# Retention, spectral mixing and a gated MLP: a new planned order, fewer warm-up products, packed state

## The chip, the cores and the metric

One NeuronCore of one Trainium2 chip runs the whole program. The metric is device microseconds of one execution; the kernel before took 392.88 us as the median of three runs (392.62 to 393.3). The engines named below are TensorE (PE, with its weight loads as PEld), VectorE (DVE), ScalarE (ACT), GpSimd (POOL) and SyncE (SP, which issues the DMAs).

## The reference, cut to what matters

All arrays are fp32. There are 2 sequences of 768 tokens, 8 heads of 64, and a model width of 512.

```
state = gamma * state + outer(k_t, v_t); y_t = scale * q_t @ state      # per head, 768 steps
theta = x @ w_theta; zr, zi = x*cos(theta), x*sin(theta)
u = x + w_tok_r @ zr + w_tok_i @ zi                                     # mixes the tokens
x2 = u + relu(u @ w_ch)
h = gelu(x2 @ w_in); a, v = halves(h)
out = x2 + (a * (w_sg @ layernorm(v) + b_sg)) @ w_out                   # w_sg mixes the tokens
```

## The kernel before, in words

**Tiling.** The retention is done in 12 chunks of 128 tokens (6 per sequence). Within a chunk the scores of all 8 heads are products of 64 rows (heads 2p and 2p+1 in the two row halves), masked by the decay on VectorE; what came before the chunk enters through a state of 64 by 64 per head. Two heads make one 128 by 128 block of `state`, of which only the two diagonal 64 by 64 blocks are filled and the rest is zero from a memset; four such blocks lie in a tile of 128 by 512, and two tiles take turns. `outer` makes the new k-v products, `grow` adds them to the state (two VectorE operations, one per half of the partitions), `fade_k` multiplies k by its decay on GpSimd and a second GpSimd product makes the faded q (`qd`). `attend` multiplies the state with `qd` (four products of 128 by 128) and adds the masked scores times v (eight products with 64 columns of weights).

**Later stages.** Each chunk then gets its angles (`theta`), cosines and sines, and joins the token mixing (`mix_main` for the first 512 tokens, `mix_rest` for the last 256). After all chunks come three dense layers over three groups of tokens: group 0 and 1 are the first 512 tokens of each sequence, group 2 the last 256 of both. In the gated MLP, `up_v`, `norm` and `up_u` run group after group; `gate_tile` of a sequence needs the normalised v of all its tokens, so of its own group and of group 2.

**Precision.** Wide products are made in three passes from a high and a low part of each operand. So every operand is split: ScalarE copies the high part (line 302), VectorE subtracts it (line 308). The 19 weight tiles come as raw 64-bit words of 1 MB; each is decoded by a ScalarE scaling (line 361), a VectorE shift (370), two VectorE passes (381), and a split. Raw tiles have two buffers (`RAWS`), so the third weight load waits until the first tile is split. fp32 products of the retention appear in the trace as two halves each; the wide products of split operands as one instruction each.

**What sets the order.** All engines run a fixed order, written by a planner (`Plan.schedule`). It keeps a clock for each engine and for the DMA queue, a price per operation, and a priority (due time); at each step it takes the engine that can start first, and on it the ready operation with the best priority among those that start within a small window (`PEL` 0.3 for TensorE). `SP` loads are priced at KB/410 us each on one queue, plus 2.0 until landing. An operation may not start more than `AHEAD` before its priority. In `C`, `SGP` says how much earlier than the first gating product the gating weights `wsg` get their priority. Operations on VectorE and GpSimd that work on SBUF alone exclude each other in the plan (`port`).

**Warm-up and fillers.** Before the planned program, 11 products of a state tile with itself are issued (`warm`). In the plan, up to 90 filler products on `ident` (`keep_warm`) are offered to TensorE; the planner puts one in where TensorE has nothing else ready, and drops those that would start after 34 us of planned time.

Where the planner starts its clocks:

```
engines = {o.eng: 0.0 for o in self.ops}
state = {"port": 0.0, "dma": 0.0, "first": 0}
```

Of the kernel before, what the change touches and what calls it, by code (L numbers as in the profile page):

```python
# [10 lines left out]
F32 = mybir.dt.float32  # L11
# [3 lines left out]
ALU = mybir.AluOpType  # L15

B, H, S, D = 2, 8, 768, 64
DM = H * D
P = 128
# [41 lines left out]
class Plan:  # L61


    LAT, AHEAD = 0.15, 45.0

    def __init__(self, room):
        self.ops, self.res, self.room = [], {}, room
# [23 lines left out]
    def schedule(self, look):  # L91


        engines = {o.eng: 0.0 for o in self.ops}

        free = {of: [0.0] * n for of, n in self.room.items()}
        rank, level = {}, {}
# [20 lines left out]
        for o in self.ops:  # L118
            if not o.missing:
                ready[o.eng].append(o)  # L120
        state = {"port": 0.0, "dma": 0.0, "first": 0}
        done = [False] * (len(self.ops) + 1)

        def earliest(o):
# [74 lines left out]
        return sorted(order, key=lambda o: (o.start, rank[o]))  # L199


C = dict(TC=13, LATE=60, AHEAD=45, LM=19, LT=2, LR=16, LW=12, LRW=0, PEL=0.3, DVEL=0.2, ACTL=0.1, CHP=5, SGP=0, RW2=1, PA=45, DEL=6, RS=6, LEAD=15, TH=0, WARM=34.0, NWARM=90)


@with_exitstack
def retention_spectral_gmlp(
# [50 lines left out]
    stats = const.tile([P, 2, 6], F32, name="stats")  # L257
    masks = const.tile([P, 2, 512], F32, name="masks")
    dk = const.tile([P, NCH, H], F32, name="dk")
    states = [const.tile([P, 512], F32, name=f"state{n}") for n in range(2)]  # L260
    for t in states:
        V.memset(t, 0.0)  # L262

    xa = [const.tile([P, NP, TA], F32, name=f"xa{b}") for b in range(B)]
    xb = const.tile([P, NP, B, TB], F32, name="xb")
# [16 lines left out]
    def mm(o, l, r, start, stop):  # L282
        nc.tensor.matmul(out=o, lhsT=l, rhs=r, start=start, stop=stop)  # L283
# [7 lines left out]
    def dve(words, fn, ps=False, fast=False, **k):  # L291
        dur = 0.15 + words * (0.52e-3 if fast else 1.042e-3)
        return plan.op("DVE", dur, fn, port=not ps, **k)

    def pool(words, fn, **k):
        return plan.op("POOL", 0.15 + words * 2.25e-3, fn, port=True, **k)
# [39 lines left out]
    def early(i):  # L336

        return max(T0 + C["RS"] * i, T(i) - C["LEAD"])

# [60 lines left out]
    def load_qk(i):  # L400
        b, c = divmod(i, NCH)
        load[i, 0] = Buf("pair")
        dma(
            512,
            lambda: nc.sync.dma_start(out=ap(load[i, 0]), in_=qkv[b, c, 0]),
            w=[load[i, 0]],
            prio=early(i) - 12,
            after=[gate[i - 3]] if i >= 3 else (),
        )
# [16 lines left out]
    def retention(i):  # L426
        b, c = divmod(i, NCH)
        t = early(i)
        load_qk(i)
        load_kv(i)  # L430
        qk, kv = load[i, 0], load[i, 1]
        if i == 0:
            dma(
                512,
                lambda: nc.sync.dma_start(out=masks, in_=dmask),
                w=["masks"],
                prio=t - 11.5,
            )
            dma(6, lambda: nc.sync.dma_start(out=dk, in_=decays), w=["dk"], prio=t - 11.2)
        sc = [bank(), bank()]  # L440

        def scores():
            q, k = ap(qk)[:, 0:512], ap(qk)[:, 512:1024]
            for p in range(NP):
                for h in range(2):
                    rows = slice(h * D, (h + 1) * D)
                    cols = slice(p * P, (p + 1) * P)
                    mm(ap(sc[h])[:, cols], k[rows, cols], q[rows, cols], True, True)

        pe(0.93, scores, r=[qk], w=sc, prio=t)  # L450
        at[i] = Buf("pair")
        for h in range(2):

            def mask(h=h):
                V.tensor_tensor(  # L455
                    out=ap(at[i])[:, h * 512 : (h + 1) * 512],
                    in0=ap(sc[h]),
                    in1=masks[:, h],
                    op=ALU.mult,
                )  # L460

            dve(512, mask, ps=True, r=[sc[h], "masks"], w=[(at[i], h)], prio=t + 1)
        if c < NCH - 1:

            def fade_k():
                k3 = ap(kv)[:, 0:512].rearrange("p (h d) -> p h d", h=H)
                G.tensor_tensor(  # L467
                    out=k3, in0=k3, in1=dk[:, c, :, None].to_broadcast([P, H, D]), op=ALU.mult
                )

            pool(512, fade_k, r=[kv, "dk"], w=[(kv, 0)], prio=t + 1)
        if c > 0:
            dq, qd = Buf(), Buf()
            dma(
                256,
                lambda: nc.sync.dma_start(out=ap(dq), in_=dqs[c - 1]),
                w=[dq],
                prio=t - 8,
                after=[gate[i - 2]] if i >= 2 else (),
            )  # L480
            pool(
                512,
                lambda: G.tensor_tensor(  # L483
                    out=ap(qd), in0=ap(qk)[:, 0:512], in1=ap(dq), op=ALU.mult
                ),
                r=[qk, dq],
                w=[qd],
                prio=t + 1.5,
            )
        state, state_next = states[c % 2], states[(c + 1) % 2]  # L490
        if c < NCH - 1:
            kp = bank()

            def outer():
                kk, vv = ap(kv)[:, 0:512], ap(kv)[:, 512:1024]
                for p in range(NP):
                    for h in range(2):
                        rows = slice(h * D, (h + 1) * D)
                        cols = slice(p * P + h * D, p * P + (h + 1) * D)
                        mm(ap(kp)[rows, cols], kk[:, cols], vv[:, cols], True, True)  # L500

            pe(0.5, outer, r=[(kv, 0), kv], w=[kp], prio=t + 2)
            for h in range(2):

                def grow(h=h):
                    rows = slice(h * D, (h + 1) * D)
                    add, old, new = (
                        x.rearrange("p (n e) -> p n e", n=NP)[rows, :, rows]
                        for x in (ap(kp), state, state_next)
                    )  # L510
                    if c == 0:
                        V.tensor_copy(out=new, in_=add)
                    else:
                        V.tensor_tensor(out=new, in0=add, in1=old, op=ALU.add)  # L514

                dve(
                    256,
                    grow,
                    ps=True,
                    r=[kp] + ([("state", c % 2, h)] if c else []),  # L520
                    w=[("state", (c + 1) % 2, h)],
                    prio=t + 2.5,
                )
        xp = bank()

        def attend():
            vv, a = ap(kv)[:, 512:1024], ap(at[i])
            if c > 0:
                for p in range(NP):
                    cols = slice(p * P, (p + 1) * P)  # L530
                    mm(ap(xp)[:, cols], state[:, cols], ap(qd)[:, cols], p == 0, False)
            for p in range(NP):
                cols = slice(p * P, (p + 1) * P)
                for h in range(2):
                    rows = slice(h * D, (h + 1) * D)
                    mm(
                        ap(xp)[rows, cols],
                        vv[:, p * P + h * D : p * P + (h + 1) * D],
                        a[:, h * 512 + p * P : h * 512 + (p + 1) * P],
                        c == 0,  # L540
                        c == 0 or p == NP - 1,
                    )

        r = [kv, (at[i], 0), (at[i], 1)]
        if c > 0:
            r += [qd, ("state", c % 2, 0), ("state", c % 2, 1)]
        gate[i] = pe(0.93 if c == 0 else 1.85, attend, r=r, w=[xp], prio=t + 3)
        keys = [("x", b, c, d) for d in range(NP)]
        act(
            512,  # L550
            lambda: A.activation(
                out=x_chunk(i),
                in_=ap(xp).rearrange("p (n t) -> p n t", n=NP),
                func=AF.Copy,
            ),
            ps=True,
            r=[xp],
            w=keys,
            prio=t + 5,
        )  # L560
        xhl[i] = pair()

        def n4(b, dtype):
            return ap(b, dtype).rearrange("p (n t) -> p n t", n=NP)

        h, l = xhl[i]
        split_hi(lambda: n4(h, F32R), lambda: x_chunk(i), 512, t + 5.5, keys, w=[h])
        split_lo(
            lambda: n4(h, F32R), lambda: n4(l, F32R), lambda: x_chunk(i), 512, t + 6, [*keys, h], [l]
        )  # L570
# [494 lines left out]
    for g in range(3):  # L1065
        for e in range(NP):
            channels(g, e, t)
            t += 2.7
    for g in range(3):
        for q in range(4):  # L1070
            up_v(g, q, t)
            t += 2.7
        norm(g, t)
        for q in range(4):
            norm_tile(g, q, t + 1)
        for f in range(NP):
            up_u(g, f, t)
            t += 2.7
# [20 lines left out]


    warm = psum.tile([P, 512], F32, tag="psum7", name="warm")
    for _ in range(11):
        mm(warm[:, 0:P], states[0][:, 0:P], states[0][:, 0:P], True, True)

    def keep_warm():
# [105 lines left out]
```

## Time and profile before

| | |
|---|---|
| median of 3 runs | 392.88 us (392.62 to 393.3) |
| profiled execution | 392.63 us, its span 390.5 us |
| TensorE busy | 383.1 us, 98% of the span |
| VectorE busy | 280.4 us, 72% |
| ScalarE busy | 167.2 us, 43% |
| GpSimd busy | 35.7 us, 9% |
| chain that ended last | TensorE 92%, VectorE 6%, issue 1% |
| granted TensorE clock | 1.00 over the whole span |

Busy times are unions of instructions of one engine. A busy TensorE is not one at its peak: products are pipelined, so each lasts longer than the time from one start to the next. In lists of single instructions, the time between the starts of two groups says how long the first one held the engine. The chain of waits follows the last instruction back to whatever released it, step by step.

### The profile page before, as it was taken

How to read it: one execution, taken by the hardware profiler on the slowest of the kernel's cores; microseconds unless marked ns; L12 is line 12 of the kernel's file. 1: busy time of each engine (PE TensorE's matmuls, PEld its weight loads, DVE VectorE, ACT ScalarE, POOL GpSimd, SP SyncE). 2: the span in 40 equal slices, each digit the busy share in tenths (PEclk: the TensorE clock that was granted, in tenths of full speed). 3: DMA queues.
4: the chain of work that ended last, by engine and by line, in shares of the span. 5: the costliest groups of instructions: out<-in, count | busy, mean ns of one | idle time of the engine just before them, and what ended most of it. 6: DMA issues, size and time to landing. Idle time of an engine off the chain costs nothing.

```text
span 390.5 us, 5822 instructions
## 1 busy us (share of the span) xinstructions
PE 383.1 (98%) x2398; PEld 328.1 (84%) x2398; DVE 280.4 (72%) x403; ACT 167.2 (43%) x240; POOL 35.7 (9%) x28
## 2 busy tenths in 40 slices
PE   8997999999999999999999999999999999999996
PEld 8986788878899988888899888888888788998885
DVE  1599998999998686869853554999998986454222
ACT  1233875548534554557132213777765821111000
POOL 1290311032014100000200000000000000000000
PEclk9999999999999999999999999999999999999999
DMA  7946664551626511308100000260000000000223
GB/s 286 415 190 217 253 277 170 186 193 55 241 104 222 215 65 44 111 0 315 77 2 0 2 0 0 85 240 1 2 0 0 2 0 1 2 0 29 107 82 107
DMA packets 11786, 41.95 MB, mean 107 GB/s; under 512 B 1520, under 2 KB 2544, under 8 KB 9328
## 3 DMA queue, kind: packets, MB, share of 16 engines
q1 hardware_dynamic: 11760, 41.58, 28.7%
q8 instruction: 19, 0.31, 0.3%
q14 instruction: 7, 0.06, 0.1%
HBM read 38.43 MB, written 3.15 MB: 106 GB/s over the span
## 4 chain that ended last, share of the span: by engine, by line
PE 92%; DVE 6%; issue 1%; ACT 0%; DVEq 0%
PE b L283 90%; DVE b L381 2%; DVE b L308 2%; PE warm L283 1%; PE b L646 1%; DVE b L370 1%; DVE b L455 0%; DVE b L611 0%; DVE b L654 0%; DVE state L514 0%; ACT b L602 0%; DVE state L262 0%; DVE b L1025 0%; DVE halfpi L251 0%; DVEq L381 0%
## 5 line engine op out<-in xcount | busy, mean ns | idle before, releaser
L283 PE MATMUL b<-b,b 128*128 128x512 f32 (+2 forms) x1788 | 332.9, 352 | 0.2 <-DVE b L308 0.2
L283 PEld LDWEIGHTS b<-b,b 128*128 128x128 f32 (+1 forms) x1788 | 277.6, 183 | 48.5 <-issue 1.4
L302 ACT ACTIVATE b<-b 128x1024 fp32r<-128x1024 f32 (+1 forms) x64 | 54.0, 864 | 67.7 <-DVE b L973 36.0
L308 DVE TENSOR_TENSOR b<-b,b 128x1024 fp32r<-128x1024 f32 (+1 forms) x64 | 62.3, 993 | 16.8 <-ACT b L302 10.7
L381 DVE SCALAR_TENSOR_TENSOR b<-b 128x1024 int32<-128x1024 int32 x38 | 50.6, 1332 | 1.3 <-ACT b L361 0.4
L361 ACT ACTIVATE b<-b 128x1024 f32<-128x1024 f32 x19 | 22.0, 1160 | 8.0 <-DVE b L455 4.9
L302 ACT ACTIVATE b<-xa 128x512 fp32r<-128x512 f32 x24 | 14.8, 628 | 22.6 <-DVE xa L775 12.0
L483 POOL TENSOR_TENSOR b<-b,b 128x512 f32<-128x512 f32 x10 | 18.7, 1867 | 61.4 <-DMA b<-dqs 61.4
L455 DVE TENSOR_TENSOR b<-b,masks 128x512 f32<-128x512 f32 x24 | 15.5, 683 | 11.6 <-PE b L283 11.5
L308 DVE TENSOR_TENSOR b<-xa,b 128x512 fp32r<-128x512 f32 x24 | 17.3, 733 | 6.5 <-ACT b L302 6.5
L787 ACT ACTIVATE b<-b 128x512 f32<-128x512 f32 x24 | 13.8, 594 | 15.4 <-PE b L283 14.8
L283 PE MATMUL b<-b 64*128 64x128 f32 (+1 forms) x352 | 20.3, 259 | 0.0
L283 PEld LDWEIGHTS b<-b 64*128 64x128 f32 (+1 forms) x352 | 17.2, 164 | 3.6 <-issue 1.7
L467 POOL TENSOR_TENSOR b<-b,dk 128x512 f32<-128x512 f32 x10 | 14.2, 1424 | 41.3 <-DMA b<-qkv 41.3
L370 DVE TENSOR_SCALAR b<-b 128x1024 int32<-128x1024 int32 x19 | 14.2, 747 | 5.0 <-DMA b<-wts 5.0
L654 DVE TENSOR_TENSOR b<-b,b 128x1024 f32<-128x1024 f32 x12 | 14.6, 1220 | 4.3 <-PE b L646 3.5
L795 DVE SCALAR_TENSOR_TENSOR b<-b,b 128x512 f32<-128x512 f32 x24 | 15.6, 673 | 2.6 <-ACT b L787 2.6
L283 PE MATMUL b<-ident 128*128 128x128 f32 x108 | 14.6, 288 | 2.5 <-DVE b L455 2.5
L811 DVE SCALAR_TENSOR_TENSOR b<-b,b 128x512 f32<-128x512 f32 x24 | 15.8, 676 | 1.4 <-ACT b L805 1.4
L283 PEld LDWEIGHTS b<-ident 128*128 128x128 f32 x108 | 13.3, 195 | 3.4 <-DVE b L455 2.7
L805 ACT ACTIVATE b<-b 128x512 f32<-128x512 f32 x24 | 14.3, 626 | 4.3 <-DVE b L795 4.3
L966 DVE SCALAR_TENSOR_TENSOR b<-b,gcol,brow 128x512 f32<-128x512 f32 x12 | 9.0, 749 | 9.6 <-PE b L283 9.6
(49 smaller groups left out, 179.8 us busy)
## 6 DMA issues: line engine op xcount, KB each, us to landing
b<-wts SPq DMA_DIRECT2D x19, 1024.0 KB, 4.9
b<-qkv SPq DMA_DIRECT2D x24, 512.0 KB, 7.0
out<-b SPq DMA_DIRECT2D x11, 256.0 KB, 2.0
b<-dqs SPq DMA_DIRECT2D x10, 256.0 KB, 5.2
b<-wsg SPq DMA_DIRECT2D x9, 256.0 KB, 6.8
masks<-dmask SPq DMA_DIRECT2D x1, 512.0 KB, 4.3
brow<-bvec SPq DMA_DIRECT2D x1, 384.0 KB, 6.9
out<-b SPq DMA_DIRECT2D x2, 128.0 KB, 1.7
```

The lines of the kernel that those rows point to most:

```text
L283: nc.tensor.matmul(out=o, lhsT=l, rhs=r, start=start, stop=stop)
L302: act(words, lambda: A.activation(out=hi(), in_=src(), func=AF.Copy), prio=prio, r=r, **k)
L308: lambda: E.tensor_tensor(out=lo(), in0=src(), in1=hi().bitcast(F32), op=ALU.subtract),
L361: lambda: A.activation(out=words(1).bitcast(F32), in_=words(1).bitcast(F32), func=AF.Copy, scale=REBIAS),
L370: lambda: V.tensor_scalar(out=words(0), in0=words(0), scalar1=29, scalar2=None, op0=ALU.logical_shift_right),
L381: lambda scalar=scalar, op=op: V.scalar_tensor_tensor(out=words(0), in0=words(1), scalar=scalar, in1=words(0), op0=op, op1=ALU.bitwise_or,),
L455: V.tensor_tensor(out=ap(at[i])[:, h * 512 : (h + 1) * 512], in0=ap(sc[h]), in1=masks[:, h], op=ALU.mult,)
L483: lambda: G.tensor_tensor(out=ap(qd), in0=ap(qk)[:, 0:512], in1=ap(dq), op=ALU.mult),
L654: V.tensor_tensor(out=z2, in0=ap(tp)[:, None, :].to_broadcast([P, 2, 512]), in1=z2, op=ALU.mult)
L795: lambda: V.scalar_tensor_tensor(out=ap(s), in0=ap(s), scalar=1.0 / GA, in1=ap(t), op0=ALU.add, op1=ALU.mult),
L805: lambda: A.activation(out=ap(s), in_=ap(s), func=AF.Tanh, scale=GA * GC),
L811: lambda: V.scalar_tensor_tensor(out=ap(o), in0=ap(s), scalar=1.0, in1=ap(t), op0=ALU.add, op1=ALU.mult),
```

## The change

It has six parts. The planner's clocks start at values set per engine and the DMA clock at 2.1 instead of all at 0 (an unused constant goes). `SGP` is 25 instead of 0. For the first chunk the multiplication of k by its decay is made on VectorE (`GP=1`). The state is packed: each partition half keeps its own 64 columns of each pair of heads, so a tile is 128 by 256, only the first one is cleared, `grow` is one operation, and the state products are eight of 64 by 64 instead of four of 128 by 128. In the gated MLP's first layer the groups come in the order 0, 2, 1. There are 8 warm-up products instead of 11.

```
+    BEGIN = {"PE": 5.2, "ACT": 2.0, "DVE": 2.0, "POOL": 1.3, "SP": 0.7}
-        engines = {o.eng: 0.0 for o in self.ops}
+        engines = {o.eng: self.BEGIN.get(o.eng, 0.0) for o in self.ops}
-        state = {"port": 0.0, "dma": 0.0, "first": 0}
+        state = {"port": 0.0, "dma": 2.1, "first": 0}
-C = dict(..., SGP=0, ...)
+C = dict(..., SGP=25, ..., GP=1)
-    states = [const.tile([P, 512], F32, name=f"state{n}") for n in range(2)]
-    for t in states:
-        V.memset(t, 0.0)
+    states = [const.tile([P, NP * D], F32, name=f"state{n}") for n in range(2)]
+    V.memset(states[0], 0.0)
 ...
+        E, eng = (V, dve) if i < C["GP"] else (G, pool)
-            pool(512, fade_k, r=[kv, "dk"], w=[(kv, 0)], prio=t + 1)
+            eng(512, fade_k, r=[kv, "dk"], w=[(kv, 0)], prio=t + 1)
 ...
-                        mm(ap(kp)[rows, cols], kk[:, cols], vv[:, cols], True, True)
+                        mm(ap(kp)[rows, p * D : (p + 1) * D], kk[:, cols], vv[:, cols], True, True)
-            for h in range(2):
-                def grow(h=h):
-                    rows = slice(h * D, (h + 1) * D)
-                    add, old, new = (
-                        x.rearrange("p (n e) -> p n e", n=NP)[rows, :, rows]
-                        for x in (ap(kp), state, state_next)
-                    )
+            def grow():
+                add = ap(kp)[:, 0 : NP * D]
+                if c == 0:
+                    V.tensor_copy(out=state_next, in_=add)
+                else:
+                    V.tensor_tensor(out=state_next, in0=add, in1=state, op=ALU.add)
 ...
-                    mm(ap(xp)[:, cols], state[:, cols], ap(qd)[:, cols], p == 0, False)
+                    for h in range(2):
+                        rows = slice(h * D, (h + 1) * D)
+                        mm(
+                            ap(xp)[rows, cols],
+                            state[rows, p * D : (p + 1) * D],
+                            ap(qd)[rows, cols],
+                            p == 0,
+                            False,
+                        )
 ...
-    for g in range(3):
+    for g in (0, 2, 1):
         for q in range(4):
             up_v(g, q, t)
 ...
-    for _ in range(11):
+    for _ in range(8):
         mm(warm[:, 0:P], states[0][:, 0:P], states[0][:, 0:P], True, True)
```

## Rows read from the trace of the kernel before

**Rows 1.** Chain of waits that ended last: start us, us, what held it.

```profile
1.47 5.07 PE warm L283 x22
...
18.70 0.71 DVE b L370
...
19.51 1.24 DVE b L381
...
20.77 1.95 DVE b L381
...
28.60 1.98 DVE b L381
...
46.87 1.65 DVE b L308
...
48.57 16.64 PE b L283 x99
...
178.22 209.17 PE b L283 x1068
```

**Rows 2.** Windows: PE, PEld, DVE, ACT, POOL busy us (instructions), clock, DMA share, GB/s.

```profile
200.00:250.00 50.00, 50.00 (x268) 43.43 (x268) 25.35 (x39) 15.39 (x25) 0.00 (x0) 1.00 0.02 6
250.00:300.00 50.00, 50.00 (x222) 41.39 (x221) 46.64 (x104) 35.38 (x61) 0.00 (x0) 1.00 0.15 59
```

**Rows 3.** Timeline to 40 us: start, length, engine, operands, count, idle before and releaser.

```profile
6.32 4.22 PE L283 MATMUL b<-ident 128*128 128x128 f32 x34
...
10.47 1.16 PE L283 MATMUL b<-b 64*128 64x128 f32 x16
...
11.67 1.29 DVE L455 TENSOR_TENSOR b<-b,masks 128x512 f32<-128x512 f32 x2 [9.71 <-PE b L283]
...
13.32 1.09 PE L283 MATMUL b<-b,b 128*64 128x128 f32 x16
...
14.25 1.73 PE L283 MATMUL b<-b 128*64 128x64 f32 x32
...
18.99 1.06 PE L283 MATMUL b<-b,state 128*128 128x128 f32 x8
...
19.52 2.11 POOL L467 TENSOR_TENSOR b<-b,dk 128x512 f32<-128x512 f32 x1 [6.96 <-DMA b<-qkv]
19.98 0.85 PEld L283 LDWEIGHTS b<-b,b 128*64 128x64 f32 x16
...
36.96 0.69 DVE L370 TENSOR_SCALAR b<-b 128x1024 int32<-128x1024 int32 x1
```

**Rows 4.** Groups by line and shape, whole span: busy us, mean ns | idle before.

```profile
L283 PE MATMUL b<-b,b 128*128 128x512 f32 x1140 | 265.5, 392 | 0.2 <-DVE b L308 0.2
...
L308 DVE TENSOR_TENSOR b<-b,b 128x512 fp32r<-128x512 f32 x33 | 21.6, 687 | 8.4 <-ACT b L302 8.4
...
L283 PE MATMUL b<-ident 128*128 128x128 f32 x108 | 14.6, 288 | 2.5 <-DVE b L455 2.5
...
L514 DVE TENSOR_TENSOR state<-b,state 64x256 f32<-64x256 f32 x16 | 6.7, 418 | 0.6 <-PE b L283 0.4
...
L1025 DVE TENSOR_TENSOR b<-b,xb 128x256 f32<-128x256 f32 x2 | 0.8, 424 | 1.8 <-PE b L283 1.8
```

**Rows 5.** Issue and landing of single loads: first q-k, first weights, third weights.

```profile
L405 SPq DMA_DIRECT2D b<-qkv x1: 382/382/382, 0.7 to 0.7; - x1
...
DMA to landing us min/median/max: 3.2/3.2/3.2
...
L348 SPq DMA_DIRECT2D b<-wts x1: 606/606/606, 4.0 to 4.0; - x1
...
DMA to landing us min/median/max: 9.4/9.4/9.4
...
L348 SPq DMA_DIRECT2D b<-wts x1: 328/328/328, 28.6 to 28.6; - x1
...
DMA to landing us min/median/max: 4.7/4.7/4.7
```

More of the change, by code (lines that the diff above doesn't have):

```diff
@@ L61 @@
 class Plan:
-    LAT, AHEAD = 0.15, 45.0
+    LAT = 0.15
+    BEGIN = {"PE": 5.2, "ACT": 2.0, "DVE": 2.0, "POOL": 1.3, "SP": 0.7}
     def __init__(self, room):
@@ L199, in schedule @@
         return sorted(order, key=lambda o: (o.start, rank[o]))
-C = dict(TC=13, LATE=60, AHEAD=45, LM=19, LT=2, LR=16, LW=12, LRW=0, PEL=0.3, DVEL=0.2, ACTL=0.1, CHP=5, SGP=0, RW2=1, PA=45, DEL=6, RS=6, LEAD=15, TH=0, WARM=34.0, NWARM=90)
+C = dict(TC=13, LATE=60, AHEAD=45, LM=19, LT=2, LR=16, LW=12, LRW=0, PEL=0.3, DVEL=0.2, ACTL=0.1, CHP=5, SGP=25, RW2=1, PA=45, DEL=6, RS=6, LEAD=15, TH=0, WARM=34.0, NWARM=90, GP=1)
 @with_exitstack
@@ L463, in retention, with fade_k @@
         if c < NCH - 1:
-            def fade_k():
+            def fade_k(G=E):
                 k3 = ap(kv)[:, 0:512].rearrange("p (h d) -> p h d", h=H)
@@ L480, in retention @@
             )
-            pool(
+            eng(
                 512,
-                lambda: G.tensor_tensor(
+                lambda: E.tensor_tensor(
                     out=ap(qd), in0=ap(qk)[:, 0:512], in1=ap(dq), op=ALU.mult
@@ L499, in outer @@
                         cols = slice(p * P + h * D, p * P + (h + 1) * D)
-                        mm(ap(kp)[rows, cols], kk[:, cols], vv[:, cols], True, True)
+                        mm(ap(kp)[rows, p * D : (p + 1) * D], kk[:, cols], vv[:, cols], True, True)
             pe(0.5, outer, r=[(kv, 0), kv], w=[kp], prio=t + 2)
-            for h in range(2):
-                def grow(h=h):
-                    rows = slice(h * D, (h + 1) * D)
-                    add, old, new = (
-                        x.rearrange("p (n e) -> p n e", n=NP)[rows, :, rows]
-                        for x in (ap(kp), state, state_next)
-                    )
[L511 to L523, printed above, removed]
+            def grow():
[4 more added lines that the diff above has]
+                    V.tensor_tensor(out=state_next, in0=add, in1=state, op=ALU.add)
+            dve(
+                256,
+                grow,
+                ps=True,
+                r=[kp] + ([("state", c % 2)] if c else []),
+                w=[("state", (c + 1) % 2)],
+                prio=t + 2.5,
+            )
         xp = bank()
@@ L530, in attend @@
                     cols = slice(p * P, (p + 1) * P)
-                    mm(ap(xp)[:, cols], state[:, cols], ap(qd)[:, cols], p == 0, False)
+                    for h in range(2):
[6 more added lines that the diff above has]
+                            False,
+                        )
             for p in range(NP):
@@ L545, in retention @@
         if c > 0:
-            r += [qd, ("state", c % 2, 0), ("state", c % 2, 1)]
+            r += [qd, ("state", c % 2)]
         gate[i] = pe(0.93 if c == 0 else 1.85, attend, r=r, w=[xp], prio=t + 3)
```

## The prediction

> **What bounds the kernel now.** I read the chain that ended last first, then the busy time by stretch, then the instructions of the first 40 us, and last the landing times of the first DMAs. The profiled execution took 392.63 us: a span of 390.5 us and 2.13 us around it. It lies 0.25 us under the median of the three runs shown (392.88), and all sums below are made against 392.63.
>
> The chain [rows 1] is TensorE alone from 48.57 us on, save the last addition: the reader sees one piece after another with no engine between, the last 209.17 us long. In the two windows cut from that stretch [rows 2] TensorE is busy for all of the 50.00 us. So after 48.57 us only fewer or shorter products can help; for those 339 us it makes no difference what VectorE does, as long as it keeps up.
>
> Before 48.57 us it is otherwise. The chain runs through VectorE while it decodes the first two weight tiles, from 18.70 to 30.6, and again just ahead of 48.57, where TensorE starts when a split of VectorE's that began at 46.87 is done [rows 1]. The early TensorE work is partly filler: 108 half-products on `ident`, 14.6 us busy [rows 4], and 22 on `state` from 1.47 to about 6.5 us. What this stage costs is thus set by when VectorE gets its first work and how long its row of conversions is. It got it late. The first q and k tile landed at 0.7 + 3.2 = 3.9 us [rows 5], but the scores made of it began at 10.47 us [rows 3], because 22 warm-up halves and 34 filler halves (6.32 to 10.47) stood ahead of them in TensorE's written order. VectorE's first mask product waited 9.71 us for those scores, until 11.67. The first weight tile landed at 4.0 + 9.4 = 13.4 us [rows 5], and VectorE began on it at 18.70 [rows 1], when the masks, splits and state additions of the first two chunks were out of its way.
>
> **The change, part by part.**
>
> *New first moments and fewer warm-up products.* The planner had TensorE free at 0, and so filled its time until its planned first landing with fillers that really ran after the warm-up. With TensorE put at 5.2 and the DMA queue at 2.1, its model of the first landing is 2.1 + 512/410 + 2.0 = 5.35, 0.15 later for the reader: nothing or a single filler fits ahead of the scores. Eight warm-up products are 16 halves; 22 took 5.07 us [rows 1], so 16 take 3.7, from about 1.2 (one memset of half the size instead of two) to 4.9. Scores(0) then begin near 5 instead of 10.47. The granted clock is 1.00 (2.4 GHz) wherever the rows show it, yet the warm-up halves took 0.23 us each and the 34 fillers behind them 0.122 (6.32 to 10.47), so the first scores may still go at the slow pace: 2 us instead of 1.1. That puts the masks near 7 instead of 11.67, and the loss of 1 us into time in which VectorE would wait for weights anyway. What VectorE owes ahead of the weights (two pairs of masks at 1.29 [rows 3]; a split and the moved multiplication at 0.69, two additions at 0.42 [rows 4]) is 4.8 us, which fits between 7 and the landing at 13.4. That landing is late next: it sits behind the loads of two chunks, the masks and the decay factors, and the change doesn't alter what is in front. I take 14.0 for VectorE's start on the weights, between the landing (13.4) and the landing plus one pair of masks (14.7). Gain: 18.70 - 14.0 = 4.7 us; both ends: 4.0 and 5.3.
>
> *Slow conversions.* After 19.5 us, when the third chunk lands and GpSimd starts on it (the multiplication that waited 6.96 us [rows 3]), VectorE's conversions are longer: the first pass took 1.24 us before GpSimd was in it, the next 1.95, and so on to 1.98 [rows 1]. The first and the last of five such pieces stand there; against 1.24 for a pass (three), 0.71 for the shift and about 1.2 for a split their excess comes to 4.2 us in all. Starting at 14.0, the first weight tile and half of the second are through before GpSimd wakes. Between nothing (the same overlap falls on later conversions) and 4.2, I take 1.0.
>
> *Packed state.* The two additions of 64x256 (0.42 each, 16 of them [rows 4], and four copies like them) become one of 128x256; the nearest row of that shape, the last addition of the kernel, took 424 ns [rows 4]. Ten times 0.42 us come off VectorE, but in the stretch that counts (18.70 to 48.57) there is one such pair: 0.4. On TensorE, eight halves of 128*128 by 128 columns took 18.99 to 19.98, 0.99 us [rows 3]; they become 16 of 64*64 by 128 columns. The nearest row is the 128*64 product with 128 columns: 16 of them from 13.32 to the next group's start at 14.25, 0.93 us, 58 ns each, half of the 124 of a full one; two halves of the array evidently work side by side. So 0.93, and one more change of shape ahead of the group, which I price at the difference of the two, 0.06: no gain, no loss. The ends: 0.06 less per chunk, and 0.17 more if the group takes as long as the 16 scores from first start to last end (1.16 [rows 3]). Seven of the ten groups lie behind 48.57 and two more in the nearly gapless stretch just before, so -0.5 to +1.5 us for the range.
>
> *First k multiplication on VectorE.* One more 128x512 product there, nearest row 0.69 us [rows 4]. It lies in VectorE's wait for the first weights and costs nothing; without that cover 0.7. GpSimd loses an operation that nobody waited on for long.
>
> *Gating weights 25 us earlier, last tokens second.* Nine loads and splits (0.69 us of VectorE each [rows 4], 6.2 together) may move out of 250 to 300 us, where VectorE is busy 46.64 of 50.00, to 200 to 250, where it is busy 25.35 [rows 2]. Their loads only move in SyncE's order there, past no transfer that TensorE waits on. TensorE doesn't wait in either stretch, so I take 0. If their buffers crowded out others, the bound is these 6.2 us; TensorE's unbroken row in both stretches leaves far less. Putting group 2 second gives the normalisation of its tokens time before the first gating product. All the waits on its splits in the run come to 0.2 us (the wide products [rows 4]): gain 0.2.
>
> Sum: 4.7 + 1.0 + 0.4 + 0.0 + 0.2 = 6.3; 392.63 - 6.3 = 386.3 us.
>
> A limit on it: the third weight tile can only be loaded when the first one's buffer is free; it was issued at 28.6 and took 4.7 us [rows 5]. Moved by 6 us it is issued at 22.6, still behind loads that the queue holds, and lands near 28. VectorE would want it near 30.7 (before: 36.96 [rows 3]). So some 2.5 us more than my sum could be gained before that transfer becomes the wait: 383.8, less at most 0.5 for the products.
>
> **The rivals.**
>
> *Given back at the next wait, 389.5.* TensorE reaches the first token mixing before the decoded weights of that step do. For it: in the stretch between the theta products and 48.57 it already waited on VectorE, 46.87 to 48.57 [rows 1], and the chunks 2 to 4 that could fill the time land no earlier than now. Against it: VectorE's whole row moves up with the start. If half of the gain turns into this wait, 392.63 - 3.1 = 389.5.
>
> *The new order doesn't start TensorE earlier, 392.4.* If the planner still puts fillers ahead of scores(0), because of its 0.3 us tie rule or because the masks' load is planned late, only 0.2 us of the normalisation's wait goes. For it: fillers are taken whenever nothing is ready. Against it: 5.2 and 5.5 leave no room for more than one. This is also the case in which the change doesn't do what it says.
>
> *The two 64*64 products don't run side by side, 395.2.* Before, the row-split scores wrote two different PSUM tiles, and the column-split ones shared a tile but used all rows. The new pair is split by rows and by columns and writes one tile: no row shows that form. If each waits for the other, 16 products go at the pace of the 128*128 ones (0.99/8 = 0.124 us): 1.98 instead of 0.99 per chunk. Nine of the ten groups lie where TensorE has no slack: 9 x 0.99 = 8.9 us, and 386.3 + 8.9 = 395.2. It decides from 0.7 us more per chunk, that is from 106 ns per product, at which my gain of 6.3 is used up. Against it stand the 58 ns of the nearest row, whose pair also shares one tile on different partitions. The Trainium skill, "TensorEngine Tiling (Array Packing)", Restrictions and Gotchas, speaks for it: different row tiles are to write to different PSUM banks and can't access the same bank at once; by that rule the time would be this rival's 395.2. The same page's Tile-to-Partition Mapping, which gives the two diagonal tiles separate partitions in PSUM, speaks for the forecast; no run here yet shows either for this form.
>
> **How the numbers follow.** Forecast 62%, with its own range 383.8 to 388.5. Better than 383.8: 5%. Half given back 16%. No earlier start 9%. Pair in series 8%. Faster by over 0.2% (under about 391.9; about what a measurement can tell from no change) are the first three, 83%; the same 9%; slower 8%. The range for 8 in 10 leaves the series case and half of the extremes out: 383.3 to 391.2.
>
> **What would show it.** Right: in the changed kernel's timeline scores(0) begin at 5 to 6 us and VectorE's first weight operation at 13.4 to 14.7; the last stretch in which the chain runs through VectorE ends at 42 to 43 instead of 48.57; fewer than 80 filler halves; 16 of the 64*64 products take 0.8 to 1.0 us from first start to the next group. Wrong: fillers still ahead of the first scores; a TensorE wait after 43 us on VectorE or on a weights' load; 64*64 products over 100 ns apart; any idle TensorE between 200 and 350 us, which would be the gating weights' doing.

## The result and the profile after

The changed kernel took 386.89 us (median of 4 runs, 386.05 to 387.6), the kernel before 392.89 (4 runs): a ratio of 0.9846, 95% interval 0.9824 to 0.9868, 6.0 us less. The forecast was 386.3 in a range of 383.3 to 391.2. The profiled execution of the changed kernel is the longest of its four, 387.6 us with a span of 385.5, so between the two profiles 5.0 us are to be found. One execution in the experiments (with the gating weights late) was disturbed, 1319.72 us, and is left out of every comparison.

The chain of waits after, start us, us, what held it, to be read against [rows 1]:

```profile
4.01 10.26 DMA b<-wts
...
14.29 1.23 ACT b L361
...
15.54 1.24 DVE b L381
...
19.96 1.98 DVE b L308
...
21.95 2.21 DVE b L381
...
42.14 1.14 DVE b L308
...
43.32 16.58 PE b L283 x107
...
176.28 206.17 PE b L283 x1056
```

From here on, "the unbroken row" is the last stretch of TensorE work, entered from VectorE's conversions, in which TensorE hardly waits. It begins at 43.32 instead of 48.57, 5.2 us sooner, and from there to its end it is nearly as long as before (339.1 us against 338.8). Ahead of it the chain no longer starts in warm-up products and fillers: it starts with the load of the first weight tile, which landed at 14.27 here, and goes from there into the conversions. This start is that of one execution: in two experiments with the same loads in the same order (the clocks alone, and three parts undone together) the tile landed earlier, and the chain runs through the load of the third chunk's q and k instead.

The timeline after, with the idle time before a group and its releaser in brackets, against [rows 3]:

```profile
4.92 1.72 PE L283 MATMUL b<-b 64*128 64x128 f32 x16
...
6.67 1.29 DVE L456 TENSOR_TENSOR b<-b,masks 128x512 f32<-128x512 f32 x2 [5.53 <-PE b L283]
...
8.62 0.69 DVE L468 TENSOR_TENSOR b<-b,dk 128x512 f32<-128x512 f32 x1 [0.66 <-DMA b<-qkv]
...
13.98 1.09 PE L283 MATMUL b<-b,state 64*64 64x128 f32 x16
...
14.29 0.70 DVE L370 TENSOR_SCALAR b<-b 128x1024 int32<-128x1024 int32 x1
...
15.01 1.09 PE L283 MATMUL b<-b,b 128*64 128x128 f32 x16
...
30.69 0.69 DVE L370 TENSOR_SCALAR b<-b 128x1024 int32<-128x1024 int32 x1
```

The scores begin at 4.92 instead of 10.47, still at the slow pace (1.72 us against 1.16), the masks at 6.67 instead of 11.67, and the first weight operation of VectorE at 14.29 instead of 18.70, 0.02 us after the landing. The third tile's shift comes at 30.69 instead of 36.96. Groups by line and shape, against [rows 4]:

```profile
L283 PE MATMUL b<-b,b 128*128 128x512 f32 x1140 | 265.0, 391 | 0.8 <-DVE b L308 0.8
...
L283 PE MATMUL b<-b,state 64*64 64x128 f32 x160 | 10.9, 275 | 0.0
L283 PE MATMUL b<-ident 128*128 128x128 f32 x76 | 10.8, 288 | 0.7 <-DVE b L456 0.7
...
L510 DVE TENSOR_TENSOR state<-b,state 128x256 f32<-128x256 f32 x8 | 3.4, 419 | 1.0 <-PE b L283 1.0
```

There are 76 filler halves instead of 108. The wide products wait 0.8 us on VectorE, all of it at 43.32, where before it was 0.2. If one adds, over all products but the warm-up and fillers, the time from each start to the next product's start, less the idle time, TensorE's real work is 364.0 us before and 364.7 after; most of the 0.7 more is the slow pace of the first scores, 0.56. What is not work (warm-up, fillers, idle, and the start up to the first product) is 23.05 us before and 17.44 after. That difference of 5.6, less the 0.7, is the 4.9 us by which the span is shorter.

### The profile page after: what moved, and what is told of

The parts are those of the page before. It is cut to its first block, busy times and chain, and to the rows that moved or that the text cites. A ratio compares the mean times of both kernels' runs of the same rounds, so it can differ in the third digit from the quotient of the medians.

```text
span 385.5 us, 5901 instructions
## 1 busy us (share of the span) xinstructions
PE 379.1 (98%) x2440; PEld 322.3 (84%) x2440; DVE 274.2 (71%) x393; ACT 167.0 (43%) x240; POOL 31.0 (8%) x27
## 3 DMA queue, kind: packets, MB, share of 16 engines
q1 hardware_dynamic: 11760, 41.58, 28.8%
## 4 chain that ended last, share of the span: by engine, by line
PE 90%; DVE 5%; DMA 3%; SPq 1%; ACT 0%; issue 0%; DVEq 0%
PE b L283 89%; DMA b<-wts 3%; DVE b L381 2%; DVE b L308 2%; PE b L650 1%; DVE b L615 0%; ACT b L361 0%; DVE b L370 0%; DVE b L658 0%; SPq L416 0%; SPq L405 0%; DVE b L456 0%; ACT b L606 0%; SPq L477 0%; DVE b L1029 0%
## 5 line engine op out<-in xcount | busy, mean ns | idle before, releaser
L308 DVE TENSOR_TENSOR b<-b,b 128x1024 fp32r<-128x1024 f32 (+1 forms) x64 | 62.0, 986 | 19.0 <-ACT b L302 10.1
L456 DVE TENSOR_TENSOR b<-b,masks 128x512 f32<-128x512 f32 x24 | 15.3, 682 | 7.9 <-PE b L283 7.8
L484 POOL TENSOR_TENSOR b<-b,b 128x512 f32<-128x512 f32 x10 | 16.0, 1596 | 53.5 <-DMA b<-dqs 53.5
L791 ACT ACTIVATE b<-b 128x512 f32<-128x512 f32 x24 | 13.8, 591 | 13.4 <-PE b L283 13.4
L815 DVE SCALAR_TENSOR_TENSOR b<-b,b 128x512 f32<-128x512 f32 x24 | 15.9, 678 | 2.8 <-ACT b L809 2.8
L606 ACT ACTIVATE b<-b 128x512 int32<-128x512 f32 x12 | 7.1, 594 | 22.9 <-PE b L283 19.6
L992 DVE TENSOR_TENSOR b<-b,xa 128x512 f32<-128x512 f32 x8 | 5.5, 690 | 14.2 <-PE b L283 14.2
L468 POOL TENSOR_TENSOR b<-b,dk 128x512 f32<-128x512 f32 x9 | 11.4, 1264 | 50.6 <-DMA b<-qkv 50.6
```

What stands on the lines that cost most here:

```text
L308: lambda: E.tensor_tensor(out=lo(), in0=src(), in1=hi().bitcast(F32), op=ALU.subtract),
L456: V.tensor_tensor(out=ap(at[i])[:, h * 512 : (h + 1) * 512], in0=ap(sc[h]), in1=masks[:, h], op=ALU.mult,)
L484: lambda: E.tensor_tensor(out=ap(qd), in0=ap(qk)[:, 0:512], in1=ap(dq), op=ALU.mult),
L815: lambda: V.scalar_tensor_tensor(out=ap(o), in0=ap(s), scalar=1.0, in1=ap(t), op0=ALU.add, op1=ALU.mult),
```

## The experiments

Each ran beside the kernel before, whose medians there were 393.17, 393.07 and 393.2 us in the three sets. Medians are compared with the changed kernel's 386.89. It was not run again in these sets, where the kernel before stood 0.2 to 0.3 us higher than beside it, and most versions ran only four or five times, 0.4 to 2.6 us apart. So a difference of some tenths between two medians shows nothing.

**The clocks at zero.** The one part that should matter, undone.

```
-    BEGIN = {"PE": 5.2, "ACT": 2.0, "DVE": 2.0, "POOL": 1.3, "SP": 0.7}
+    BEGIN = {}
-        state = {"port": 0.0, "dma": 2.1, "first": 0}
+        state = {"port": 0.0, "dma": 0.0, "first": 0}
```

> The changed kernel with the planner's engine and DMA clocks back at 0; all other parts of the change stay, the 8 warm-up products too. In the written order 17 filler products stand ahead of the first scores again (as before the change), against none in the changed kernel. If the late first scores were what cost the time, most of the gain goes: first scores near 9.3 us (3 warm-up products fewer than before, 0.7 to 1.1 us), VectorE's first weight operation near 17.5, end at 391 to 392. Rival (the gain comes from the packed state or the layer order): stays at 387 to 388.

Measured: 392.26 us, ratio to the kernel before 0.9984 (0.9959 to 1.0009). Its timeline and chain:

```profile
1.20 3.78 PE L283 MATMUL warm<-state 128*128 128x128 f32 x16 [1.20 <-DVE state L262]
4.77 5.01 PE L283 MATMUL b<-ident 128*128 128x128 f32 x34
9.71 1.16 PE L283 MATMUL b<-b 64*128 64x128 f32 x16
```

```profile
18.38 0.61 DVE b L370
...
48.63 16.58 PE b L283 x107
```

The 34 filler halves stand ahead of the scores again, which begin at 9.71; the weights wait until 18.38, though their load had long landed, and the unbroken row begins at 48.63. With every other part of the change in place, 5.4 of the 6.0 us are gone; beside the kernel before of its own set the interval takes in no change.

**The clocks alone.** The kernel before with the new clocks and eight warm-up products.

```
+    BEGIN = {"PE": 5.2, "ACT": 2.0, "DVE": 2.0, "POOL": 1.3, "SP": 0.7}
+        engines = {o.eng: self.BEGIN.get(o.eng, 0.0) for o in self.ops}
+        state = {"port": 0.0, "dma": 2.1, "first": 0}
+    for _ in range(8):
```

> The kernel before with the new clocks and 8 warm-up products alone: wide state, old layer order, old gating weights' priority, first k multiplication on GpSimd. If the first moments carry the gain: 387 to 388 (the 0.4 us of state additions and 0.2 us of the gating wait missing against 386.9). Rival (the packed state or the other parts carry half of it): 389.5 or more.

Measured: 387.29 us, ratio 0.9844 (0.9809 to 0.9879), the same as the whole change. The first weight tile landed at 13.62 us in its profile, VectorE began on it at 13.64, and TensorE enters its long row at 41.65. Two waits on VectorE break that row, 0.68 us at 90.49 and 0.36 at 301.56, just ahead of the gating:

```profile
41.65 16.66 PE b L284 x99
...
90.49 13.52 PE b L284 x84
...
301.56 80.14 PE b L284 x431
```

So the first moments carry the gain by themselves, and the two runs together leave nothing large for the rest. Which of the new start values does it was not tried one by one; in the plan it is TensorE's 5.2 that leaves no room for fillers ahead of a first landing at 5.5.

**Wide state.** The changed kernel with the state as it was, in `outer`, `grow` and `attend`.

```
-    states = [const.tile([P, NP * D], F32, name=f"state{n}") for n in range(2)]
+    states = [const.tile([P, 512], F32, name=f"state{n}") for n in range(2)]
...
-            def grow():
+            for h in range(2):
+                def grow(h=h):
```

> The changed kernel with the state as before: blocks of 128 by 128, two tiles cleared, two additions per chunk, four 128 by 128 products. By the prediction this costs VectorE 0.4 us in the first stage, 0.42 per chunk later where it is hidden, and the first warm-up product 0.25 us, and nothing on TensorE: 387.2 to 387.8. Rival (VectorE's 4.2 us of saved additions all count): 390 to 391. Rival (the narrow products are dearer than they look): 386 or less.

Measured: 386.41 us (385.69 to 388.05), ratio 0.9827 (0.9791 to 0.9862). The expected 0.3 to 0.9 us of loss are not there, but the runs lie 2.4 us apart, so a loss or a gain of that size can't be told. What they rule out is that all of the 4.2 us that the packed state saves on VectorE count: most of them lie beside other work.

**Pairs in series.** The same 64 by 64 products, the upper half's four first.

```
-                for p in range(NP):
-                    for h in range(2):
+                for h in range(2):
+                    for p in range(NP):
                         mm(ap(xp)[rows, cols], state[rows, p * D : (p + 1) * D], ap(qd)[rows, cols], p == 0, False)
```

> The changed kernel with the eight 64 by 64 state products of a chunk issued half by half (all four of the upper half, then all four of the lower) instead of in turn, so that neighbours use the same quarter of the array. Same products, same count, same planned order. If two quarters work side by side only when neighbours differ, a group of 16 takes 1.7 to 2.0 us instead of 1.0 and the run is 6 to 9 us longer: 393 to 396. If pairs never ran side by side, or if the engine finds the other quarter's products further back, the time stays at 386.9 within 0.5.

Measured: 391.26 us, ratio 0.9945 (0.9925 to 0.9964), 4.4 us more than the changed kernel. A group and its successor on TensorE:

```profile
13.22 1.58 PE L283 MATMUL b<-b,state 64*64 64x128 f32 x16
14.73 1.09 PE L283 MATMUL b<-b,b 128*64 128x128 f32 x16
```

From start to start 1.51 us, against 1.03 in the changed kernel (13.98 to 15.01): 0.48 per group, 4.8 for ten. All ten groups of either kernel show it (1.02 and 1.51 us, idle time left out). The single starts in the traces tell how. In turn, the two products of a pair start 6 or 7 ns apart and the next pair mostly 102 or 103 ns later, so a pair takes the 109 ns that one product takes alone. Half by half, the first four and the last four follow one another at 109 ns, and only the middle ones come closer, many of them at 52 to 57. So products of the two diagonal quarters do overlap, though both write one PSUM tile, and more than half of what that saves is lost when they are not taken in turn. I expected 1.7 to 2.0 and 6 us or more, which is what no overlap at all would give; the half-by-half order takes 94 ns per product. (This profile also has a wait of 1.09 us at 138.18, of the kind told below under eleven warm-up products.)

**Gating weights, layer order and first multiplication undone together.** `SGP=0`, `for g in range(3)`, `GP=0` in the changed kernel.

> The changed kernel with three of its parts undone together: gating weights' priority as before, layer groups in the order 0, 1, 2, and the first k multiplication back on GpSimd. Prediction: 0.2 to 0.3 us of a wait before the first gating product comes back and nothing else: 386.9 to 387.3. Rival (one of them is needed to keep TensorE fed once the first stage is shorter): 388 or more, with idle TensorE between 200 and 310 us.

Measured: 387.96 us, ratio 0.9872 (0.9856 to 0.9888), 1.1 more than the changed kernel. Before the first gating product TensorE waits, which it does not in the changed kernel (one piece of 46 products from 295.69 to past 306):

```profile
301.21 0.50 PE L283 MATMUL b<-b,b 128*128 128x512 f32 x1 [0.18 <-ACT b L302]
302.52 1.66 PE L283 MATMUL b<-b,b 128*128 128x512 f32 x6 [0.80 <-DVE b L308]
```

That is 0.98 us, against the 0.2 that I had counted for it, and close to the whole difference of the medians. What it waits for is the split of the normalised v (lines 302 and 308).

**Layer order 0, 1, 2 alone.**

```
-    for g in (0, 2, 1):
+    for g in range(3):
```

> The changed kernel with the layer groups in the order 0, 1, 2 again, all else kept. In the run with three parts undone TensorE waited 0.98 us on a split just before the first gating product (301 to 302.5 us). If the order of the groups is what keeps that wait away, it is here again: 387.4 to 388.2, with 0.3 to 1.0 us of idle TensorE near 300 us. Rival (the earlier gating weights do it): no wait there and 386.9.

Measured: 388.01 us (387.37 to 389.98), ratio 0.9865 (0.9848 to 0.9881). In its profile the wait at 304 to 305 us is there again, 0.34 + 0.22 us:

```profile
304.05 0.50 PE L283 MATMUL b<-b,b 128*128 128x512 f32 x1 [0.34 <-ACT b L302]
304.77 1.43 PE L283 MATMUL b<-b,b 128*128 128x512 f32 x5 [0.22 <-DVE b L308]
```

All three readable profiles with the old order and the early start have it (0.36, 0.98 and 0.56 us), and none of the nine with the new order. So the order of the groups keeps the gating wait away: with the old order the wait stands with the gating weights early (here) and late (the other two). The rest of the 1.1 us is within the spread of the runs.

**Gating weights late, alone.** `SGP=0` in the changed kernel.

> The changed kernel with the gating weights' priority as before the change, all else kept. If the earlier gating weights keep TensorE fed before the first gating product: idle TensorE of 0.3 to 1 us near 300 us and 387.4 to 388.2. Rival (the order of the groups does it, and the weights' splits have cover in either place): 386.9 within 0.5.

Measured: 385.45, 386.87 and 388.91 us, ratio 0.9847 (0.9807 to 0.9888), and no profile to set beside the others. Inconclusive: what the earlier gating weights do by themselves stays open.

**Eleven warm-up products.** `for _ in range(11)` in the changed kernel, the plan untouched.

> The changed kernel with 11 warm-up products instead of 8; the plan is untouched. The first scores begin 6 x 0.21 = 1.3 us later (6.2 instead of 4.9). If the landing of the first weight tile sets VectorE's start (14.3 in the changed kernel's profile), the 1.3 us vanish in VectorE's wait: 386.9 within 0.5. If the start of the scores sets the time, as I argued for the kernel before: 388.2.

Measured: 387.78 us, ratio 0.9869 (0.9854 to 0.9883), 0.9 more, between the two expectations. Its profile has two losses. The first is at the start. The first weight tile landed early, at 13.32 us, and VectorE came to it only at 14.55, 1.2 us later, held up by the second chunk's masks, state addition and split; the chain of this profile starts in the warm-up products and the scores, not in the load:

```profile
1.20 5.06 PE warm L283 x22
6.26 5.43 PE b L283 x78
```

```profile
14.55 0.69 DVE L370 TENSOR_SCALAR b<-b 128x1024 int32<-128x1024 int32 x1
```

The row then begins at 42.98, against 41.92 and 41.65 in the profiles of the two experiments where the tile landed nearly as early (13.76 and 13.62). The second loss stands at 135.20. A VectorE split that took 1.22 us there in the changed kernel met a GpSimd product that began ahead of it, at 130.17, and took 2.32, and TensorE waited for the addition behind it:

```profile
130.40 2.32 DVE L308 TENSOR_TENSOR b<-b,b 128x1024 fp32r<-128x1024 f32 x1
132.64 0.68 DVE L737 TENSOR_TENSOR xb<-b,xb 128x512 f32<-128x512 f32 x1
```

```profile
135.20 2.09 PE L283 MATMUL b<-b,b 128*128 128x512 f32 x8 [1.09 <-DVE xb L737]
```

So later scores do cost VectorE time when the load lands early, and are covered by it when it lands late; that is the changed kernel's case in its profile (14.27). The second loss is a matter of how two engines happen to meet: TensorE waits for the same addition in three other profiles, 0.33 us with the clocks at zero, 1.09 with the pairs in series, 0.19 with the layer order alone, and not in the changed kernel's. How the 0.9 us divides over the two is not shown; all four runs lie above 387.6.

**Loads of the first weights moved forward.** The chain after begins with that load, so four placings of it were tried, each by one constant in the changed kernel (`TH` is added to the priority of the first two weight tiles).

```
-C = dict(..., TH=0, ...)
+C = dict(..., TH=-13, ...)      # weights ahead of all loads; -9, -11 and -12.2 for the others
```

Both tiles between the first and the second chunk (-9):

> The changed kernel with the first two weight tiles 9 us earlier in priority, so that their loads are issued after the first chunk's k and v and ahead of the second chunk's. The first weight tile should land near 10 to 11 instead of 13.4 to 15.3. If that landing is what now bounds the first stage, VectorE starts on the weights 3 us earlier and up to 3 us are gained: 384 to 385.5. Rival (the second chunk, which lands later by 2 MB or 5 us, leaves TensorE and VectorE with nothing, or VectorE's row of conversions only gets the masks behind instead of ahead of them): 386.5 to 388.

Measured: 386.87 us, ratio 0.9841 (0.9825 to 0.9858). The first after the first masks, the second after k and v (-11):

> The first weight tile's load after the first chunk's q and k and the masks, but ahead of its k and v; the second after these. Landing near 8 and 12. If time follows the landing of the first tile one for one once it is late, this lies between the version with the weights first (385.4) and the changed kernel (386.9): 385.5 to 386.5. Rival (what matters is the whole burst, which ends at 26 us in any order): 386.9.

Measured: 386.76 us, ratio 0.9841 (0.9826 to 0.9856). The first tile ahead of everything, the second behind the masks (-12.2):

> The first weight tile's load ahead of all others, then the first chunk's q and k and the masks, then the second weight tile. The version with both weight tiles first ran at 385.4. Here VectorE gets masks 2.5 us sooner and the second tile 2.5 us later. If VectorE's row of work is the bound as soon as it has any weights, 384.5 to 385.5; if the second tile's landing (near 10) or the later order decides, 385.5 to 387.

Measured: 386.78 us, ratio 0.9840 (0.9825 to 0.9855). Both tiles ahead of everything (-13):

> The changed kernel with the first two weight tiles 13 us earlier, their loads ahead of everything else. They should land near 5.5 and 8, the first q and k near 9.5, the last chunk of the first load burst no later than now. If VectorE's row of work is the bound, it fills its time from 6 us on with weights instead of waiting for scores, and 3 to 5 us are gained: 382 to 384. Rival (the chunks' own chain from q and k to the first angles, now starting 5.5 us later, becomes the wait): 386 to 389.

Measured: 385.38 us (385.2 to 386.17), ratio 0.9809 (0.9794 to 0.9823): 7.7 us under the kernel before and 1.5 under the changed kernel, the fastest version here. VectorE's first weight operation, 0.03 us after the landing, and TensorE's start on real work:

```profile
5.49 0.71 DVE L370 TENSOR_SCALAR b<-b 128x1024 int32<-128x1024 int32 x1 [4.34 <-DMA b<-wts]
```

```profile
10.33 1.16 PE L283 MATMUL b<-b 64*128 64x128 f32 x16
```

The first tile landed at 10.28, 8.95, 5.53 and 5.46 us in the profiles of the four versions, in the order told here. So the landing of the weights, which heads the chain, is not by itself what decides: three versions have it 4 to 9 us earlier and gain nothing that can be told from the spread. Their profiles show what waits in its place. With -9 and -11 (in this order below) TensorE waits for the third chunk's q and k, which land when they did before, at 18.20 and 18.78 us against 18.39 in the changed kernel, and the chain of both runs through that load:

```profile
18.33 1.16 PE L283 MATMUL b<-b 64*128 64x128 f32 x16 [0.38 <-DMA b<-qkv]
```

```profile
18.91 1.16 PE L283 MATMUL b<-b 64*128 64x128 f32 x16 [1.23 <-DMA b<-qkv]
```

With -12.2 TensorE waits for no load, but its waits and fillers after 30 us come to 2.2 us, against 0.8 in the changed kernel. The fastest has the scores 5 us later than the changed kernel and loses nothing by it: VectorE converts weights in the meantime, TensorE waits for no load, and the scores go at the full pace (1.09 us from first start to the next group instead of 1.65). Summed as above, what is not work is 15.9 us there against 17.4, and the work 364.3 against 364.7. All four versions have a wait on VectorE of 0.3 to 0.7 us at 77 to 79 us that the changed kernel does not have. How much of the missing gain each of these takes was not tested.

## Why the prediction was right, point by point

**The bound.** It named the late scores, behind fillers that the planner had put there by a wrong clock. The two runs with the clocks show it from both sides: with the clocks at zero, 392.26; with the clocks alone, 387.29.

**The sum.** 6.3 us was forecast and 6.0 measured between the medians, but the profiles, which alone can be set against the terms, lie 4.9 us apart in span. TensorE's first theta product comes 5.8 us sooner, its unbroken row 5.2, its end 4.9. So the terms up to the theta products hold, a part is given back behind them that the sum had not taken off, and the last term was not there. That the median came within 0.6 us of 386.3 is partly luck: the profiled execution is the slowest of the four.

**The first moments (4.7 us).** VectorE's start on the weights was put at 14.0 and is 14.29: 4.4 us. The scores (near 5), the masks (near 7), the slow pace of the first products and the landing of the first tile as what is late next all came so. What the range of 13.4 to 14.7 did not take in is that this landing varies: 13.4 before, 14.3 in the changed kernel's profile, 15.3 in two of the experiments, with the same loads issued ahead of it. The loss to the slow pace, put at 1 us, was 0.56 in this profile; over the profiles of versions whose scores begin near 4.9 us they took 1.09 to 2.01 us to the next group, so this term moves from execution to execution.

**Slow conversions (1.0).** From VectorE's first weight operation to TensorE's first theta product the kernel before took 18.70 to 36.20, the changed one 14.29 to 30.44: 1.35 us less, of which the single state addition is up to 0.4. So about 1.0, as taken. Up to the theta products VectorE has three long pieces while GpSimd works (2.07, 2.29 and 1.52 us, from 19.88 on); before there were five (1.95, 1.78, 1.87, 2.29 and 2.06, from 20.77 on). No experiment took GpSimd out of the way, so the cause is read from this overlap alone.

**What is left of it at the end of the stage.** Some 0.6 us is lost again where TensorE enters its unbroken row: it waits 0.8 us there on VectorE, 0.2 before. The row begins at 43.32; I had said 42 to 43, and I had named a wait of TensorE on VectorE after 43 us as a sign of being wrong. This is the rival "given back at the next wait" in small, a tenth of the gain instead of half.

**Packed state (0.4, and nothing on TensorE).** The group of 16 takes 1.03 us, just outside the 0.8 to 1.0 that I gave, against 0.99 of the 8 full halves [rows 3]; summed with their changes of shape 160 take 10.2 us and the 80 took 10.1. So nothing on TensorE, as said. The 0.4 on VectorE was not found by undoing it, nor could it have been within that spread.

**Layer order (0.2).** This term was mis-sized, and read from the wrong row: the 0.2 us in [rows 4] is the wait at 48.57. Before the first gating product of the kernel before, the weight load waited 0.42 us (at 307.31 us) and TensorE's record shows no gap. So the new order took no TensorE wait away between the two profiles. In the shortened kernel the old order costs 0.4 to 1.0 us of waits. Read in the trace of before, a wait says what it costs there, not what it costs when its neighbours move.

**The rival of pairs in series (8%).** It would have decided from 106 ns per product. They go at 64 ns each in turn. The Trainium skill's rule, in "TensorEngine Tiling (Array Packing)", Restrictions and Gotchas, that different row tiles can't use one PSUM bank at a time, does not hold for the diagonal pair here: both products write one PSUM tile, and they start 6 or 7 ns apart. The same page's Tile-to-Partition Mapping gives the two diagonal tiles PSUM partitions 0 to 63 and 64 to 127. The trace fits that: the pairs run side by side.

**The limit by the third tile's load.** It was issued at 21.98 (near 22.6 expected) and landed at 28.8; VectorE came to it at 30.69. It did not bind.

## What to carry to other kernels

Where an order is written out from a model, compare the model's first moments with the trace's: here four to five microseconds of fillers stood ahead of the first real products because the plan believed an engine free that was still warming up, and putting the plan's clocks right gave nearly all of the 6.0 us. A part that takes work from an engine off the path, as the packed state does, gains little by itself: 4.2 us less on VectorE gave nothing that the runs could tell. Before moving a load forward because it heads the chain, ask what it displaces: four placings of the same two tiles gave 0 to 1.5 us, and none gave what the landing alone promised.

## What the runs showed of the hardware that was not expected

A load issued at the same moment behind the same loads (the first weight tile at 4.0 us) landed between 13.3 and 15.3 us in the profiled executions. Whether that is what spreads the times of the kernels that wait for it is not shown: the changed kernel ran at 386.05 to 387.6, but the kernel before, which does not wait for it, at up to 395.29 in the experiments.

Pairs of 64 by 64 products on diagonal quarters of the array share a PSUM tile without waiting for each other: in turn a pair takes as long as one of them alone.

The granted clock of 1.00 over the whole span is not shown for the first microseconds. The clock record in the traces begins at 6.9 us before and 6.1 us after (4.5 to 7.3 over the profiled executions that have one), at the 2.4 GHz level, after TensorE had run warm-up products since 1.47 and 1.20 us; earlier time has no record, and the views count it as full. TensorE's pace rises at about that moment: the warm-up halves took 0.23 us each, the fillers behind them 0.122.
